# Attention of a three-layer kernel: chunks of 64 on quarter tiles, transposed output placed by copies, first loads by tensor

## The chip, the cores and the metric

One core of a Trainium2 chip runs the kernel. The time is the device time of one execution in microseconds (us). The engines are PE (TensorE, matrix products, with its weight loads shown apart as PEld), DVE (VectorE), ACT (ScalarE), POOL (GpSimd) and SP (SyncE, which issues all DMAs here).

## The reference

Three layers follow each other. The first is a gated linear attention with a state of 48 x 48 per head (4 batches, 8 heads, 768 steps); the other two are dense layers on its output, 3072 tokens of 384 values.

```
f = 1 / (1 + exp(-f_logit))
for t in range(768):
    state = f[:, :, t, :, None] * state + outer(k[:, :, t], v[:, :, t])
    y[:, :, t] = q[:, :, t] @ state
x = y, heads side by side                    # 3072 x 384
x = (h * tanh(softplus(h))) @ w_out          # h = x @ w_in, 384 -> 2048 -> 384
out = (sigmoid(x @ w_gate) * (x @ w_val)) @ w_out2   # 384 -> 1536 -> 384
```

The weights come as 64-bit floats and are turned into pairs of 32-bit parts on the chip; the inputs q, k, v, f as 32-bit.

## The kernel before, in words

**Attention.** A unit is four heads (two pairs, r = 0 and 1; in a pair one head lies on partitions 0 to 47, the other on 64 to 111) over half a sequence, 384 steps. There are 16 units; units 2j and 2j+1 make the x of block j, a block being 384 tokens. `unit(m)` (line 404) puts a unit's steps on a calendar of ticks: loads (`load_qkf`, `load_v`), the exponential of the forget logits and +1 (`s_exp`), the running product R of 1/f within a chunk of 128 steps by scans on VectorE (`s_scan`, six instructions), its logarithm and inverse on ScalarE (`s_lnexp`), the scaling of k and q by R and its inverse (`s_hat`), the scores of each chunk on PE (`p_scores`, per r) and their causal mask on VectorE (`s_mask`), the transposes of k (`p_kt`) and their copy out of PSUM (`s_kt`), the state that each chunk adds (`p_state`), the scan that carries it over chunks (`s_state`), the state's part of the output (`p_inter`), the chunk's own part (`p_intra`), and the copy of the output into `xtok`, tokens on partitions (`s_out`, lines 535 to 542).

**First dense layer.** `block1(j)` transposes `xtok` on PE (`p_xt`, nine 128 x 128 transposes a block), copies the result out of PSUM on ScalarE (`s_xt`), splits x into a high and a low part (`s_x`), and then does 16 hidden slices of 128: nine main products each into the hidden layer (`p_h`, tile h) and, 11 ticks later, nine out of it (`p_o`, tiles y0 to y2, from ghi and glo). Each main product is a 128 x 128 weight tile with 384 moving columns. One hidden slice is one tick; a block is 16 ticks. ScalarE evicts h and computes the activation in groups of four slices, VectorE helps.

**Weights.** `weights1` (line 643) loads and converts w_in in pairs of slices (buffers hs2, ghi1, glo1, z) and w_out in single slices (stg0, stg1, both): one or two ScalarE and four VectorE instructions each (`conversion`). `weights2` converts the second layer's weights between ticks 27 and 110 into DRAM (w2d) and loads them again when room is free. `block2` is the last layer.

**Order.** Every step has a tick and a priority (`at`). A planner (`_in_order`, with `_cost` for durations) fixes the order of all instructions from them: on each engine, the step that is ready and has the smallest (tick, priority) goes first. At run time each engine, and SP with all its DMAs, keeps that order. T0[m] is unit m's tick: -13, -9, 0, 4, then 8m - 23. All recorded instructions have line 926.

Of the kernel before, what the change touches and what calls it, by code (L numbers as in the profile page):

```python
# [20 lines left out]
C = 128  # L21
T = 384
# [70 lines left out]
def _cost(engine, method, args, kwargs):  # L93
# [215 lines left out]
def kernel(  # L309
# [53 lines left out]
    def flat(tag, n, dt=F32):  # L363

        return st(tag, [128, n if tag == "S" else 2 * T], dt)[:, 0:n]

# [8 lines left out]
    rb = st("rb", [128, 1])  # L375
# [3 lines left out]
    sc = st("sc", [128, 2, 2, D])  # L379
# [12 lines left out]
    def setup():  # L392
        nc.scalar.preload_act_table_set("natural_log_exp_and_others")
        nc.gpsimd.memset(rb.get(), RBIG)
# [3 lines left out]
        nc.gpsimd.affine_select(out=cm.get(), in_=cm.get(), pattern=[[1, C]], compare_op=ALU.is_ge, fill=0.0, base=0, channel_multiplier=-1)  # L398
        nc.vector.memset(fl.get(), 0.0)


    xtok = {}

    def unit(m):
# [8 lines left out]
        tR, tpf, *tA, tkt, tT = EARLY[m] if m < len(EARLY) else LATER  # L413
# [7 lines left out]
        def load_qkf():  # L421
            u["qkf"] = st(f"qkf{m % 2}", [128, 2, 3, T])
            sp.dma_start(out=u["qkf"], in_=qkf[n0 : n0 + 2].rearrange("r p i t -> p r i t"))
            u["q"], u["k"], u["f"] = (u["qkf"][:, :, i, :] for i in range(3))

        def load_v():
            u["vn"] = st("vn", [128, 2, T // 128, 2 * D])
            sp.dma_start(out=u["vn"], in_=vn[n0 : n0 + 2].rearrange("r p i d -> p r i d"))

        def s_exp():  # L430
            f = u["f"]
            act.activation(out=f, in_=f, func=AF.Exp, scale=-1.0)
            dve.tensor_scalar(out=f, in0=f, scalar1=1.0, scalar2=None, op0=ALU.add)
# [15 lines left out]
        def s_hat():  # L449
# [7 lines left out]
            pz = u["pz"] = flat("v6" if m == 1 else "S", 2 * D * NC).rearrange("p (r e c) -> p r e c", r=2, c=NC)  # L457
            pool.memset(pz[:, :, :, 0], 0.0)
            act.activation(out=pz[:, :, :, 1:NC], in_=pend[:, :, 0 : NC - 1].unsqueeze(2).to_broadcast([128, 2, D, NC - 1]), func=AF.Copy)

        def p_scores(r):
            ps = u["ps", r] = pst(pq, "s", [128, 2, 512])
            for i in range(NC):
                t = slice(i * C, (i + 1) * C)
                for hd, (_, rows_) in enumerate(heads):
                    pe.matmul(ps[:, hd, t], u["k"][rows_, r, t], u["q"][rows_, r, t], start=True, stop=True)

        def s_mask(r):
            A = u["A", r] = flat(tA[r], 2 * T).rearrange("p (h i t) -> p h i t", h=2, t=C)
            dve.tensor_tensor(  # L470
                out=A, in0=u["ps", r][:, :, 0:T].rearrange("p h (i t) -> p h i t", t=C),
                in1=cm.unsqueeze(1).unsqueeze(1).to_broadcast([128, 2, NC, C]), op=ALU.mult,
            )

        def p_kt(r):
            ps = u["pk", r] = pst(pa, "a", [128, T])
# [8 lines left out]
        def p_state():  # L485
            ps = u["pu"] = pst(pa, "a", [128, T])
            cols = ps[:, 0 : 2 * NC * D].rearrange("p (r e c) -> p r e c", r=2, c=NC)
            if half:
                for r in range(2):
                    pe.matmul(cols[:, r, :, 0], ident, sc[:, pp, r, :], start=r == 0, stop=False)  # L490
            for r in range(2):
                for i in range(NC):
                    for hd, (h, _) in enumerate(heads):
                        pe.matmul(
                            cols[h, r, :, i], u["kt"][:, r, C * i + 64 * hd : C * i + 64 * hd + 64], u["vn"][:, r, i, D * hd : D * hd + D],
                            start=not half and r == i == 0, stop=r == 1 and i == NC - 1,
                        )

        def s_state():
            n = 2 * NC * D  # L500
            t = u["t"] = flat(tT, n)
            dve.tensor_tensor_scan(
                out=t, data0=u["pz"].rearrange("p r e c -> p (r e c)"), data1=u["pu"][:, 0:n], initial=0.0, op0=ALU.mult, op1=ALU.add
            )
            t = u["t"] = t.rearrange("p (r e c) -> p r e c", r=2, c=NC)
            S = u["S"] = flat("S", 2 * (NC - 1) * D).rearrange("p (r c e) -> p r c e", r=2, e=D)
            dve.tensor_tensor(
                out=S, in0=t.rearrange("p r e c -> p r c e")[:, :, 0 : NC - 1, :],
# [3 lines left out]
        def s_carry():  # L512
            dve.tensor_tensor(
                out=sc[:, pp], in0=u["t"][:, :, :, NC - 1], in1=pend[:, :, NC - 1 : NC].to_broadcast([128, 2, D]), op=ALU.mult
            )

        todo = [(i, r) for r in range(2) for i in range(NC)]

        def p_inter():
            ps = u["py"] = pst(pq, "s", [128, 2, 512])  # L520
            inter = [x for x in todo if half or x[0]]
            for i, r in inter:
                for hd, (_, rows_) in enumerate(heads):
                    S = u["S"][rows_, r, i - 1, :] if i else sc[rows_, pp, r, :]
                    o = slice((2 * i + r) * D, (2 * i + r + 1) * D)
                    pe.matmul(ps[:, hd, o], u["q"][rows_, r, i * C : (i + 1) * C], S, start=(i, r) == inter[0], stop=False)

        def p_intra(r):
            ps = u["py"]
            for i in range(NC):  # L530
                for hd in range(2):
                    o = slice((2 * i + r) * D, (2 * i + r + 1) * D)
                    pe.matmul(ps[:, hd, o], u["A", r][:, hd, i, :], u["vn"][:, r, i, D * hd : D * hd + D], start=False, stop=(i, r) == todo[-1])

        def s_out():
            if pp == 0:
                xtok[j] = st("xtok", [128, T // 128, DM])
            to = xtok[j][:, :, 4 * D * pp : 4 * D * (pp + 1)].rearrange("p i (r h e) -> p i r h e", r=2, h=2)
            for hd in range(2):
                act.activation(  # L540
                    out=to[:, :, :, hd], in_=u["py"][:, hd, 0 : 2 * NC * D].rearrange("p (i r e) -> p i r e", r=2, e=D), func=AF.Copy, scale=-1.0,
                )

        o = OFFS[0 if m < 2 else 1 if m < 4 else 2]
        at(t0 - 4, 0, load_qkf)
        at(t0 + o[3], 0, load_v)
# [4 lines left out]
        at(t0 + o[4], 50, lambda: p_scores(0))  # L551
        at(t0 + o[4], 51, lambda: p_kt(0))
        at(t0 + o[4], 51.1, lambda: s_mask(0))
        at(t0 + o[4], 51.2, lambda: s_kt(0))
        at(t0 + o[5], 50, lambda: p_scores(1))
        at(t0 + o[5], 50, lambda: p_kt(1))
        at(t0 + o[5], 51.1, lambda: s_mask(1))
# [3 lines left out]
        late = 0 if m < 4 else 2  # L561
# [3 lines left out]
        at(t0 + o[8] + 0.5 * late, 52, lambda: p_intra(0))  # L565
        at(t0 + o[8] + late, 52, lambda: p_intra(1))
# [117 lines left out]
    xt, xf, xh, xl = {}, {}, {}, {}  # L684
# [6 lines left out]
    def block1(j):  # L691
        t0 = NF1 * j

        def p_xt(kc):
            ps = xt[j, kc] = pst(pa, "a", [128, T])
            for i in range(T // 128):
                t = slice(i * 128, (i + 1) * 128)
                pe.transpose(ps[:, t], xtok[j][:, i, kc * 128 : kc * 128 + 128], ident)

        def s_xt(kc):  # L700
            if kc == 0:
                xf[j] = st("y1s", [128, KC, T])
            act.activation(out=xf[j][:, kc, :], in_=xt[j, kc], func=AF.Copy)

# [7 lines left out]
        for kc in range(KC):  # L712
            at(t0 - 3 + kc, 54, lambda kc=kc: p_xt(kc))
            at(t0 - 2 + kc, 1, lambda kc=kc: s_xt(kc))
# [286 lines left out]
```

## Time and profile before

| | |
|---|---|
| median of 3 runs | 1049.8 us (1049.34 to 1050.55) |
| profiled execution | 1050.13 us, span 1048.4 us |
| PE busy in the span | 1006.4 us, 5922 matrix instructions |
| DVE, ACT busy | 519.2 and 541.3 us |
| DMA | 93.81 MB, 89 GB/s in the mean |

The profile is one execution. The span runs from its first to its last instruction, and the execution's own time is 1.7 us longer. Matrix products are pipelined and overlap; the time from one entry of the chain of waits to the next is what a step costs.

### The profile page before, as it was taken

To read this page: it belongs to the slowest core of one execution; us is meant where nothing else is said; L and a number is where in the kernel's file an instruction comes from. 1 tells how busy PE (TensorE), PEld (TensorE's weight loads), DVE (VectorE), ACT (ScalarE), POOL (GpSimd) and SP (SyncE) were. 2 spreads that over 40 slices of the span, in tenths; PEclk is the share of its full clock that TensorE was granted. 3 is DMA by queue.
4 is the path that set the end of the run, shared out by engine and by line. 5 is a ranking of instruction groups with operands and counts; after the bars stand their busy time and mean duration, and the time that the engine had idled before them with its cause. 6 is when DMAs were issued, how large, how long until landed. Compare 5 with 4: busy or idle time off the path is not lost.

```text
span 1048.4 us, 14376 instructions
## 1 busy us (share of the span) xinstructions
PE 1006.4 (96%) x5922; PEld 898.3 (86%) x5922; DVE 519.2 (50%) x806; ACT 541.3 (52%) x778; POOL 30.5 (3%) x44
## 2 busy tenths in 40 slices
PE   0799999999999999999999999999999999999996
PEld 0789999999999999999999888888888888888885
DVE  7789997786777878763333222222121121221221
ACT  5369888878787888766678312122122122211121
POOL 0000000000000000000011001001001001000000
PEclk9999999999999999999999999999999999999999
DMA  8225334544254444410247221001000000000001
GB/s 341 87 73 188 107 102 141 177 144 151 99 184 149 159 161 147 170 46 13 88 151 230 90 65 63 1 14 48 1 31 31 1 30 1 1 31 1 1 31 33
DMA packets 40041, 93.81 MB, mean 89 GB/s; under 512 B 3872, under 2 KB 15648, under 8 KB 39968
## 3 DMA queue, kind: packets, MB, share of 16 engines
q1 hardware_dynamic: 39968, 92.81, 26.1%
q8 instruction: 48, 0.79, 0.3%
q14 instruction: 25, 0.20, 0.1%
HBM read 69.21 MB, written 23.59 MB: 89 GB/s over the span
## 4 chain that ended last, share of the span: by engine, by line
PE 88%; DVE 5%; DMA 3%; ACT 2%; issue 1%; SPq 0%; DVEq 0%
PE y L926 31%; PE h L926 31%; PE s L926 18%; PE a L926 8%; DMA stg<-in_w_dram 2%; ACT z L926 1%; DMA w2d<-stg 1%; DVE w L926 1%; DVE v L926 1%; DVE hs L926 1%; DVE stg L926 0%; DVE qkf L926 0%; DMA hs<-in_w_dram 0%; DVE glo L926 0%; DVE R L926 0%
## 5 line engine op out<-in xcount | busy, mean ns | idle before, releaser
L926 PE MATMUL y<-ghi,v 128*128 128x384 f32 (+1 forms) x948 | 282.0, 352 | 0.0
L926 PE MATMUL h<-xs,w 128*128 128x384 f32 (+1 forms) x1260 | 255.3, 347 | 0.0
L926 ACT ACTIVATE hs<-h 128x384 f32<-128x384 f32 (+1 forms) x200 | 104.8, 524 | 288.1 <-PE h L926 287.3
L926 PEld LDWEIGHTS h<-xs,w 128*128 128x128 f32 x1260 | 220.1, 189 | 5.4
L926 PEld LDWEIGHTS y<-ghi,v 128*128 128x128 f32 x948 | 174.7, 188 | 11.0
L926 PE MATMUL y<-glo,v 128*128 128x384 f32 (+1 forms) x474 | 164.5, 347 | 0.0
L926 ACT ACTIVATE ghi<-hs 128x512 fp32r<-128x512 f32 (+1 forms) x104 | 87.9, 889 | 87.8 <-PE y L926 83.1
L926 DVE TENSOR_TENSOR glo<-hs,ghi 128x512 fp32r<-128x512 f32 (+1 forms) x104 | 101.7, 1015 | 60.9 <-ACT ghi L926 59.3
L926 DVE TENSOR_TENSOR hs<-hs,s 128x512 f32<-128x512 f32 x48 | 33.0, 687 | 168.4 <-PE s L926 151.6
L926 ACT ACTIVATE z<-z 128x1536 f32<-128x1536 f32 x64 | 94.9, 1482 | 14.0 <-DVE z L926 13.7
L926 PEld LDWEIGHTS y<-glo,v 128*128 128x128 f32 x474 | 89.1, 188 | 4.3
L926 DVE SCALAR_TENSOR_TENSOR hs<-z,hs 128x1536 f32<-128x1536 f32 x32 | 56.2, 1756 | 60.9 <-ACT z L926 60.9
L926 DVE TENSOR_TENSOR hs<-hs,a 128x512 f32<-128x512 f32 x24 | 16.5, 688 | 128.1 <-PE a L926 123.0
L926 PE MATMUL y<-ghi,w 128*128 128x512 f32 x180 | 60.5, 394 | 0.0
L926 PE MATMUL s<-qkf 48*128 48x128 f32 x384 | 33.6, 313 | 26.9 <-DVE qkf L926 25.8
L926 PEld LDWEIGHTS s<-qkf 48*128 48x128 f32 x384 | 27.0, 208 | 34.5 <-DVE qkf L926 25.8
L926 ACT ACTIVATE z<-z,fifth 128x1536 f32<-128x1536 f32 x32 | 50.3, 1571 | 0.2
L926 ACT ACTIVATE z<-hs 128x1536 f32<-128x1536 f32 x32 | 47.6, 1488 | 0.7
L926 PEld LDWEIGHTS s<-vn,A 128*128 128x128 f32 x360 | 46.4, 201 | 0.0
L926 DVE TENSOR_SCALAR z<-z 128x1536 f32<-128x1536 f32 x32 | 30.9, 965 | 29.8 <-ACT z L926 29.5
L926 PE MATMUL s<-vn,A 128*128 128x48 f32 x360 | 45.1, 279 | 0.0
L926 PEld LDWEIGHTS y<-ghi,w 128*128 128x128 f32 x180 | 33.8, 188 | 7.9
(244 smaller groups left out, 1404.5 us busy)
## 6 DMA issues: line engine op xcount, KB each, us to landing
qkf<-in_qkf_dram SPq DMA_DIRECT2D x16, 1152.0 KB, 5.3
stg<-in_w_dram SPq DMA_DIRECT2D x36, 384.0 KB, 3.2
w2d<-stg SPq DMA_DIRECT2D x36, 384.0 KB, 2.8
w<-w2d SPq DMA_DIRECT2D x16, 384.0 KB, 4.1
v<-w2d SPq DMA_DIRECT2D x14, 384.0 KB, 3.1
vn<-in_vn_dram SPq DMA_DIRECT2D x16, 288.0 KB, 3.2
y1d<-y1s SPq DMA_DIRECT2D x24, 192.0 KB, 2.7
stg<-in_w1o_dram SPq DMA_DIRECT2D x11, 384.0 KB, 3.8
```

Source lines behind the costliest of these rows:

```text
L926: issue(*map(_now, args), **{k: _now(x) for k, x in kwargs.items()})
```

## The change

Chunks are 64 steps rather than 128, so a unit has six per half sequence and row pair. Two neighbouring chunks (even and odd, `h`) lie in the two halves of the partitions. Every attention product works on 64 rows and 64 columns of the array, in an `order` in which successive products go to different quarters (inter: two of them in turn).

- `s_scan` is two scans instead of six; the restart at a chunk's first step comes from `m2`, into which ScalarE writes the first 1+exp(-f) of each chunk.
- Scores of both r share one PSUM tile, with one mask instruction.
- The state is copied out of PSUM by ScalarE, the carried state is added on VectorE rather than by identity products on PE, and the scan runs over 576 elements rather than 288.
- `p_inter` and `p_intra` give the output transposed (head dimension on partitions, steps along the row); weights of 64 columns reach 16 past a head's 48, for which zeros are kept (`s_pad`, one small identity product and a copy).
- `s_out` evicts the output transposed and puts each head's rows into `xf` by SP copies inside SBUF, five per unit, a head that crosses 128 rows in two. `p_xt` and `s_xt` go.
- q, k and f of a unit are three loads. For units 0 and 1 they are early: f0, k0, q0, f1, then the first weight pair, then k1, q1 and v; the other weight loads come after that. Unit 1 uses the PSUM tiles y0 to y2 and h, and +1 is on ScalarE for these two units.
- Later units start one tick later (8m - 22), and the wait between inter and intra is one tick rather than two.

```diff
-C = 128
+C = 64
...
-T0 = [-13, -9, 0, 4] + [8 * m - 23 for m in range(4, ND)]
-LATER = ("R", "pf", "A0", "A1", "pf", "R")
-EARLY = [("R", "pf", "A0", "A1", "v15", "v14"), ("v7", "v8", "v9", "v10", "v11", "v12"), LATER[:4] + ("v13", "v14"), LATER[:4] + ("v12", "v15")]
+T0 = [-13, -9, 0, 4] + [8 * m - 22 for m in range(4, ND)]
+LATER = ("R", "pf", "A0", "pf")
+EARLY = [LATER[:3] + ("v15",), ("v7", "v8", "v9", "v10"), LATER[:3] + ("v13",), LATER[:3] + ("v12",)]
...
-        rows_, cols = aps[1].shape
-        return 0.225 if rows_ == cols == 128 else 0.07 if rows_ == 128 else 0.145 if n == 128 else 0.125
+        return 0.035 if aps[1].shape[0] < 128 else 0.1
...
+        order = [(i, hd, h) for i in range(T // 128) for hd, h in ((0, 0), (1, 1), (0, 1), (1, 0))]
+        tR, tpf, tA, tkt = EARLY[m] if m < len(EARLY) else LATER
...
+        def load_qkf(part=None):
+            if part in (None, 2):
+                u["qkf"] = st(f"qkf{m % 2}", [128, 3, 2, T])
+                u["q"], u["k"], u["f"] = (u["qkf"][:, i] for i in range(3))
+            for i in (2, 1, 0) if part is None else (part,):
+                sp.dma_start(out=u["qkf"][:, i], in_=qkf[n0 : n0 + 2, :, i].rearrange("r p t -> p r t"))
...
+            act.activation(out=m2[:, :, :, 0], in_=chunks(f)[:, :, :, 0], func=AF.Identity, bias=1.0)
+            if m < 2:
+                act.activation(out=f, in_=f, func=AF.Identity, bias=1.0)
+            else:
+                dve.tensor_scalar(out=f, in0=f, scalar1=1.0, scalar2=None, op0=ALU.add)
...
+        def banks(kind):
+
+            if m == 1:
+                ps = [pst(py, f"y{i}", [128, T]) for i in range(2)] if kind != 1 else [pst(ph, "h", [128, T]) for i in range(2)]
+                return ps, None
+            ps = pst(pq, "s", [128, 2, 512])
+            return [ps[:, i, 0:T] for i in range(2)], ps[:, :, 0:T]
+
+        def both(ps, fn):
+
+            if ps[1] is not None:
+                fn(ps[1], slice(0, 2))
+            else:
+                for i in range(2):
+                    fn(ps[0][i].unsqueeze(1), slice(i, i + 1))
+
+        def bank():
+            return pst(py, "y2", [128, T]) if m == 1 else pst(pa, "a", [128, T])
...
-                for c in range(NC):
-                    t = slice(c * C, (c + 1) * C)
-                    dve.tensor_tensor_scan(
-                        out=u["R"][:, r, t], data0=u["f"][:, r, t], data1=rb.to_broadcast([128, C]), initial=1.0, op0=ALU.mult, op1=ALU.min
-                    )
+                dve.tensor_tensor_scan(
+                    out=u["R"][:, r], data0=u["f"][:, r], data1=m2[:, r].rearrange("p c t -> p (c t)"), initial=1.0, op0=ALU.mult, op1=ALU.min
+                )
...
+        def p_scores():
+            ps = u["ps"] = banks(0)
+            for r in range(2):
+                for i, hd, h in order:
+                    rows_ = heads[hd][1]
+                    t = slice((2 * i + h) * C, (2 * i + h + 1) * C)
+                    o = slice((3 * r + i) * C, (3 * r + i + 1) * C)
+                    pe.matmul(ps[0][hd][heads[h][0], o], u["k"][rows_, r, t], u["q"][rows_, r, t], start=True, stop=True)
+
+        def s_mask():
+            A = u["A"] = flat(tA, 2 * T).rearrange("p (h x t) -> p h x t", h=2, t=C)
+            both(u["ps"], lambda ps, hd: dve.tensor_tensor(
+                out=A[:, hd], in0=ps.rearrange("p h (x t) -> p h x t", t=C),
+                in1=cm.unsqueeze(1).unsqueeze(1).to_broadcast([128, hd.stop - hd.start, NC, C]), op=ALU.mult,
+            ))
...
+            ps = u["pu"] = banks(1)
+            for i, hd, h in order:
                 for r in range(2):
-                    pe.matmul(cols[:, r, :, 0], ident, sc[:, pp, r, :], start=r == 0, stop=False)
-            for r in range(2):
-                for i in range(NC):
-                    for hd, (h, _) in enumerate(heads):
-                        pe.matmul(
-                            cols[h, r, :, i], u["kt"][:, r, C * i + 64 * hd : C * i + 64 * hd + 64], u["vn"][:, r, i, D * hd : D * hd + D],
-                            start=not half and r == i == 0, stop=r == 1 and i == NC - 1,
-                        )
+                    o = slice((3 * r + i) * D, (3 * r + i + 1) * D)
+                    pe.matmul(
+                        ps[0][h][heads[hd][0], o], u["kt"][heads[h][0], r, 128 * i + 64 * hd : 128 * i + 64 * hd + 64],
+                        v_(h, r, i, hd)[:, 0:D], start=True, stop=True,
+                    )
+
+        def v_(h, r, i, hd):
+
+            a = (2 * (3 * r + i) + hd) * D
+            return u["vn"][heads[h][0], a : a + 64]
...
+            t = u["f"].rearrange("p r t -> p (r t)")[:, 0:n]
+            cols = t.rearrange("p (e x h) -> p h x e", h=2, x=NC)
+            both(u["pu"], lambda ps, h: act.activation(
+                out=cols[:, h], in_=ps[:, :, 0 : NC * D].rearrange("p h (x e) -> p h x e", e=D), func=AF.Copy
+            ))
+            T_ = u["t"] = t.rearrange("p (e r c) -> p e r c", r=2, c=NC)
+            was = sc[:, 0 : 4 * D].rearrange("p (a r e) -> p a e r", a=2, r=2)[:, pp]
+            if half:
+                dve.tensor_tensor(out=T_[:, :, :, 0], in0=T_[:, :, :, 0], in1=was, op=ALU.add)
+            dve.tensor_tensor_scan(out=t, data0=u["pz"].rearrange("p e r c -> p (e r c)"), data1=t, initial=0.0, op0=ALU.mult, op1=ALU.add)
...
+            ps = u["py"] = banks(2)
+            begun = set()
+            for r in range(2):
+                for i, hd, h in order:
+                    c = 2 * i + h
+                    if c or half:
+                        o = slice((3 * r + i) * C, (3 * r + i + 1) * C)
+                        t = slice(c * C, (c + 1) * C)
+                        pe.matmul(ps[0][h][heads[hd][0], o], S_(hd, r, c), u["q"][heads[hd][1], r, t], start=(h, hd) not in begun, stop=False)
+                        begun.add((h, hd))
+            u["0"] = bank()[:, 0 : 64 - D]
+            pe.matmul(u["0"], ident, sc[:, 4 * D :], start=True, stop=True)
+
+        def s_pad():
+            dve.tensor_copy(out=u["vn"][:, 4 * T // 128 * D :], in_=u["0"])
...
+            for r in (1, 0):
+                for i, hd, h in order[::-1]:
+                    o = slice((3 * r + i) * C, (3 * r + i + 1) * C)
+                    pe.matmul(
+                        ps[0][h][heads[hd][0], o], v_(h, r, i, hd), u["A"][heads[h][0], hd, 3 * r + i, :],
+                        start=False, stop=r == i == 0,
+                    )
...
-                xtok[j] = st("xtok", [128, T // 128, DM])
-            to = xtok[j][:, :, 4 * D * pp : 4 * D * (pp + 1)].rearrange("p i (r h e) -> p i r h e", r=2, h=2)
-            for hd in range(2):
-                act.activation(
-                    out=to[:, :, :, hd], in_=u["py"][:, hd, 0 : 2 * NC * D].rearrange("p (i r e) -> p i r e", r=2, e=D), func=AF.Copy, scale=-1.0,
-                )
+                xf[j] = st("xf", [128, KC, T])
+            xT = rows(flat(tA, 2 * T))
+            cols = xT.rearrange("p r (i h t) -> p h (r i) t", h=2, t=C)
+            both(u["py"], lambda ps, h: act.activation(
+                out=cols[:, h], in_=ps.rearrange("p h (x t) -> p h x t", t=C), func=AF.Copy, scale=-1.0
+            ))
+            for r in range(2):
+                for hd in range(2):
+                    a = (4 * pp + 2 * r + hd) * D
+                    e = 0
+                    while e < D:
+                        kc, row = divmod(a + e, 128)
+                        n = min(D - e, 128 - row)
+                        sp.dma_start(out=xf[j][row : row + n, kc, :], in_=xT[64 * hd + e : 64 * hd + e + n, r, :])
+                        e += n
...
+        if m < 2:
+            for i, tick in ((2, -21 + m / 10), (1, -20.99 + 0.94 * m), (0, -20.98 + 0.94 * m)):
+                at(tick, 0, lambda i=i: load_qkf(i))
+            at(-20.04 + m / 100, 0, load_v)
+        else:
+            at(t0 - 4, 0, load_qkf)
+            at(t0 + o[3], 0, load_v)
...
+        at(t0 + o[8], 54, s_pad)
+        at(t0 + o[8] + late, 55 if m < 4 else 52, p_intra)
...
-        pairs = {t: (-20 + i / 10, e) for i, (t, e) in enumerate((("hs2", 15), ("ghi1", 9), ("glo1", 11), ("z", 2.5)))}
-        singles = {t: (-19 + i / 10, 99) for i, t in enumerate(("stg0", "stg1", "both"))}
+        pairs = {t: (-20.5 + i, e) for i, (t, e) in enumerate((("hs2", 15), ("ghi1", 9), ("glo1", 11), ("z", 2.5)))}
+        singles = {t: (-18 + i / 10, 99) for i, t in enumerate(("stg0", "stg1", "both"))}
...
-        def p_xt(kc):
-            ps = xt[j, kc] = pst(pa, "a", [128, T])
-            for i in range(T // 128):
-                t = slice(i * 128, (i + 1) * 128)
-                pe.transpose(ps[:, t], xtok[j][:, i, kc * 128 : kc * 128 + 128], ident)
-
-        def s_xt(kc):
-            if kc == 0:
-                xf[j] = st("y1s", [128, KC, T])
-            act.activation(out=xf[j][:, kc, :], in_=xt[j, kc], func=AF.Copy)
```

## Rows read from the trace of the kernel before

**Rows 1.** The page: busy time of each engine, then tenths in 40 slices.

```profile
PE 1006.4 (96%) x5922; PEld 898.3 (86%) x5922; DVE 519.2 (50%) x806; ACT 541.3 (52%) x778; POOL 30.5 (3%) x44
...
PE   0799999999999999999999999999999999999996
...
DVE  7789997786777878763333222222121121221221
...
GB/s 341 87 73 188 107 102 141 177 144 151 99 184 149 159 161 147 170 46 13 88 151 230 90 65 63 1 14 48 1 31 31 1 30 1 1 31 1 1 31 33
```

**Rows 2.** Stage busy us: PE, PEld, DVE, ACT, POOL; clock, DMA share, GB/s.

```profile
0.00:64.00 64.00, 31.58 (x213) 27.66 (x214) 50.08 (x89) 29.89 (x47) 1.73 (x13) 1.00 0.54 199
64.00:124.90 60.90, 60.90 (x495) 57.47 (x495) 55.64 (x94) 50.19 (x75) 0.70 (x3) 1.00 0.33 109
124.90:171.00 46.10, 46.10 (x324) 44.72 (x323) 41.42 (x70) 40.59 (x58) 0.23 (x1) 1.00 0.44 152
100.00:300.00 200.00, 200.00 (x1466) 191.84 (x1466) 165.48 (x271) 166.72 (x239) 1.57 (x6) 1.00 0.42 142
```

**Rows 3.** The chain of waits at the start: start us, us, what.

```profile
25.75 1.68 PE s L926 x12
...
64.13 6.15 PE h L926 x27
```

**Rows 4.** The start in order of time: start us, us, engine, line, operation.

```profile
4.28 1.03 SPq L926 DMA_DIRECT2D qkf<-in_qkf_dram  x2
...
16.20 0.83 ACT L926 ACTIVATE qkf<-qkf 128x768 f32<-128x768 f32 x1
...
18.34 1.99 DVE L926 TENSOR_TENSOR_SCAN R<-qkf,rb 128x128 f32<-128x128 f32 x6
```

**Rows 5.** PE in order of time, 50 to 70 us.

```profile
52.55 5.35 PE L926 MATMUL s<-vn,v 128*128 128x48 f32 x24
```

**Rows 6.** The chain of waits between 205 and 300 us.

```profile
206.12 0.87 PE s L926 x12
206.98 1.79 PE y L926 x9
208.77 0.33 PE a L926 x3
...
215.17 1.21 PE a L926 x28
...
221.28 1.57 PE h L926 x9
...
224.43 1.47 PE s L926 x24
...
229.24 1.27 PE s L926 x12
...
252.67 0.84 PE a L926 x24
...
257.18 1.02 PE s L926 x16
```

**Rows 7.** VectorE and ScalarE by shape: busy us, mean ns of one.

```profile
L926 DVE TENSOR_TENSOR_SCAN R<-qkf,rb 128x128 f32<-128x128 f32 x90 | 30.4, 403 | 0.0
L926 DVE TENSOR_TENSOR A<-s,cm 128x768 f32<-128x768 f32 x30 | 28.6, 952 | 5.5 <-PE s L926 5.4
...
L926 DVE TENSOR_TENSOR_SCAN R<-S,a 128x288 f32<-128x288 f32 x12 | 9.0, 747 | 3.6 <-PE a L926 3.6
...
L926 ACT ACTIVATE hs<-h 128x384 f32<-128x384 f32 x128 | 61.7, 482 | 34.2 <-PE h L926 33.4
```

**Rows 8.** DMA issues: KB each, median us from issue to landing.

```profile
y1d<-y1s SPq DMA_DIRECT2D x24, 192.0 KB, 2.7
...
hs<-in_w_dram SPq DMA_DIRECT2D x4, 768.0 KB, 4.5
...
out_dram<-z SPq DMA_DIRECT2D x12, 64.0 KB, 1.7
```

More of the change, by code (lines that the diff above doesn't have):

```diff
@@ L374 @@
     cm = st("cm", [128, C])
-    rb = st("rb", [128, 1])
+    m2 = st("m2", [128, 2, NC, C])
     fifth = st("fifth", [128, 1])
@@ L393, in setup @@
         nc.scalar.preload_act_table_set("natural_log_exp_and_others")
-        nc.gpsimd.memset(rb.get(), RBIG)
+        nc.gpsimd.memset(m2.get(), RBIG)
+        nc.gpsimd.memset(sc.get(), 0.0)
         nc.gpsimd.memset(fifth.get(), 0.2)
@@ L419, in rows @@
             return ap.rearrange("p (r t) -> p r t", r=2)
[L421 to L424, printed above, removed]
+        def load_qkf(part=None):
[4 more added lines that the diff above has]
+                sp.dma_start(out=u["qkf"][:, i], in_=qkf[n0 : n0 + 2, :, i].rearrange("r p t -> p r t"))
         def load_v():
-            u["vn"] = st("vn", [128, 2, T // 128, 2 * D])
-            sp.dma_start(out=u["vn"], in_=vn[n0 : n0 + 2].rearrange("r p i d -> p r i d"))
+            n = 4 * T // 128 * D
+            u["vn"] = flat("v5" if m == 1 else "vn", n + 64 - D)
+            sp.dma_start(out=u["vn"][:, 0:n].rearrange("p (r i d) -> p r i d", r=2, d=2 * D), in_=vn[n0 : n0 + 2].rearrange("r p i d -> p r i d"))
         def s_exp():
@@ L456, in s_hat @@
             dve.tensor_scalar(out=pend, in0=chunks(pf)[:, :, :, C - 1], scalar1=-1.0, scalar2=None, op0=ALU.mult)
-            pz = u["pz"] = flat("v6" if m == 1 else "S", 2 * D * NC).rearrange("p (r e c) -> p r e c", r=2, c=NC)
+            pz = u["pz"] = flat("v6" if m == 1 else "S", 2 * D * NC).rearrange("p (e r c) -> p e r c", r=2, c=NC)
             pool.memset(pz[:, :, :, 0], 0.0)
-            act.activation(out=pz[:, :, :, 1:NC], in_=pend[:, :, 0 : NC - 1].unsqueeze(2).to_broadcast([128, 2, D, NC - 1]), func=AF.Copy)
-        def p_scores(r):
-            ps = u["ps", r] = pst(pq, "s", [128, 2, 512])
-            for i in range(NC):
[L464 to L472, printed above, removed]
-            )
+            act.activation(out=pz[:, :, :, 1:NC], in_=pend[:, :, 0 : NC - 1].unsqueeze(1).to_broadcast([128, D, 2, NC - 1]), func=AF.Copy)
+        def p_scores():
[12 more added lines that the diff above has]
+            ))
         def p_kt(r):
-            ps = u["pk", r] = pst(pa, "a", [128, T])
+            ps = u["pk", r] = bank()
             for i in range(T // 128):
@@ L499, in s_state, with S_ @@
+        def v_(h, r, i, hd):
+            a = (2 * (3 * r + i) + hd) * D
+            return u["vn"][heads[h][0], a : a + 64]
+        def S_(hd, r, c):
+            a = (5 * r + c - 1) * D if c else (2 * pp + r) * D
+            return (u["S"] if c else sc)[heads[hd][1], a : a + 64]
         def s_state():
             n = 2 * NC * D
[L501 to L504, printed above, removed]
@@ L513, in s_carry @@
             dve.tensor_tensor(
-                out=sc[:, pp], in0=u["t"][:, :, :, NC - 1], in1=pend[:, :, NC - 1 : NC].to_broadcast([128, 2, D]), op=ALU.mult
+                out=sc[:, 0 : 4 * D].rearrange("p (a r e) -> p a e r", a=2, r=2)[:, pp], in0=u["t"][:, :, :, NC - 1],
+                in1=pend[:, :, NC - 1].unsqueeze(1).to_broadcast([128, D, 2]), op=ALU.mult,
             )
-        todo = [(i, r) for r in range(2) for i in range(NC)]
         def p_inter():
[L520 to L526, printed above, removed]
@@ L560, in unit @@
         at(t0 + o[7], 2, s_state)
-        late = 0 if m < 4 else 2
+        late = 0 if m < 4 else 1
         at(t0 + o[8], 52, p_inter)
@@ L798, in load_y @@
         def load_y():
-            two = st("xtok", [128, 2, T2])
+            two = st("xf", [128, 2, T2])
             yf[j] = [two[:, 0], two[:, 1], st("y1s", [128, T2])]
@@ L809, in s_ysplit @@
                 else:
-                    parts[j] = [st(tag, [128, T2], F32R) for tag in ("R", "pf", "A0", "A1", "stg0", "stg1")]
+                    parts[j] = [st(tag, [128, T2], F32R) for tag in ("R", "pf", "A0", "m2", "stg0", "stg1")]
             yh[j, kc], yl[j, kc] = parts[j][2 * kc : 2 * kc + 2]
```

44 lines of the change are left out of this document (13 added, 31 removed).

## The prediction

> **What bounds the kernel now.** I read the page first. PE is busy for 96% of the span, with slices of 0 and 7 tenths at the start and 9 from then on; VectorE stands at 7 to 9 tenths through most of the first half and then falls to 3 and less [rows 1]. So there is a start without main products, a long stretch bound by PE with little to spare beside it, and a second half with PE alone. The stage table prices this: VectorE works 50.1 of the first 64 us while PE has 31.6, and from 64 us on PE is busy for all of each stretch [rows 2]. The chain of waits gives the border: the first product of the first hidden layer (PE h) begins at 64.1 us, and PE's first work of all, scores, only at 25.75 [rows 3].
>
> Why so late? In order of time the two qkf loads are issued at 4.28, behind six weight loads. Unit 0's exponential comes at 16.20, its running product (R) at 18.34 [rows 4]. The page's first slice moves 341 GB/s [rows 1]; the six weight loads (3 x 768 and 3 x 384 KB, 3.5 MB) and one qkf load (1.2 MB) need 13.8 us at that, so 16.2 is about when q, k and f of unit 0 can be in.
>
> All of this start runs with PE at the lower of its two levels, 1.2 GHz. The granted-clock column says 1.00 even there [rows 2], but the durations don't: 24 intra-chunk instructions take 5.35 us at 52.55, twelve take 1.27 later, 223 against 106 ns each [rows 5, 6].
>
> **PE, per unit (16 units of four heads).** One fp32 call is two MATMUL instructions in the trace: six calls show as x12. Steady prices [rows 6]: scores 2 x 0.87; k transposes 2 x 0.33; state 0.84 without and 1.21 with the carried state, mean 1.03; products of the state into the output (inter) 1.02 and 1.47, mean 1.25; intra 2 x 1.27. The nine transposes of x in a block are 3 x 0.33, so 0.5 per unit. The group of nine main products behind small tiles takes 1.79 in place of 1.57: 0.2 each after scores (twice), state and inter. Sum 8.5 us. A block has 32 groups of nine, 50.2 us at 1.57, and two units: 67.2 us.
>
> Afterwards scores, state and intra are 24 calls each, 48 instructions on 64 rows and 64 columns, and four quarters of the array take turns. No row shows a quarter. The nearest is state, 128 rows by 64 columns on two halves: 24 in 0.84, 35 ns each, so a half comes round every 70 ns. If a quarter comes round in the same 70, four give 17.5 ns: 0.84 per step. The upper end is the row itself, 35: 1.68. I take 17.5, because the moving width grows only from 48 to 64 while the number of tiles doubles. Inter uses two quarters only, since a head's rows of S and of its output lie on the same partitions: 44 instructions in the mean at 35 ns, 1.54; ends 17.5 (0.77) and 61 ns (1.47/24, two row groups with 128 columns: 2.7). The pad product is one more call, priced as one of the two that make 1.21 of 0.84: 0.19. k transposes stay, 0.66; four switches of 0.2, 0.8; the transposes of x go. Sum 3 x 0.84 + 1.54 + 0.19 + 0.66 + 0.8 = 5.7, so 2.8 us less per unit; with both ends, from 3.6 less to 0.9 more.
>
> The Trainium skill speaks against this halving: "TensorE: Matmul & The Clock Gate", section "Wait — 56ns, not 53.3ns?", says that start to start never drops below about 25 ns however small N is. No row here goes below 35, so none contradicts it. By that figure three steps would be an estimated 48 x 0.025 = 1.2 each, and a unit would lose 1.7 rather than 2.8.
>
> **VectorE and ScalarE, per unit** [rows 7]. VectorE: the mask is one instruction of 0.95 rather than two, -0.95; R two scans for six over the same elements, 2 x (403 + 256 x 2.15 = 953 ns) for 1.99 [rows 4], -0.1; the state scan has 576 for 288 elements at (747-403)/160 = 2.15 ns, +0.62; S 288 elements more at the mask's 1.24 ns, +0.36; adding the carried state (every other unit) and the pad copy, two small ones, +0.3. Net +0.2. ScalarE, at 482/384 = 1.26 ns an element: the state out of PSUM, 576 elements, +0.72; the pz broadcast, 288 more, +0.36; the first column of each chunk and 192 output elements more, +0.4; evictions of x, 1.5 x 0.48 less. Net +0.7 at most. Between 100 and 300 us ScalarE has 166.7 of 200, VectorE 165.5 [rows 2]: 28.0 of 33.6 per unit for ScalarE, then 28.7 of 30.8. Hidden, but tight; I charge 3 us in total for lost cover, between 0 and half of the steady gain.
>
> **Moved loads and copies.** Each unit's output is placed by five SBUF-to-SBUF copies, and qkf comes in three loads for one: seven more issues on SP, 0.5 us each (two in 1.03 [rows 4]), 3.5 us per 30 of a queue that holds w2 loads and stores behind them. Each copy waits there for ScalarE's eviction, and a late w2 load would show as VectorE waiting for stg. No row has such a copy; 1.7 us (64 KB to DRAM) and 4.5 (768 KB in) bound it, and the 192 KB store's 2.7 is nearest in kind [rows 8]. A unit's output comes at tick 8m-12, the split that reads it at tick 16j, so the later unit has four ticks, at 3.8 us each, for 3 us of copies: covered. At the start alone, for unit 1, it is on the path, in place of three rounds of transpose and eviction ahead of the h products at 64.13 [rows 3]; I count it even.
>
> **The start.** f of unit 0 goes first: 384 KB is 1.15 us at 341 GB/s, on top of the 2.2 that a 768 KB load of 4.5 has besides its transfer [rows 8], so it lands at about 4.2. Then the exponential and +1 on ScalarE (0.83 each [rows 4]) to 6; two scans to 7.9; the products with R (0.95 each, as the mask), with unit 1's scans among them: scores at about 13.5 rather than 25.75. From there four PE steps per unit at half speed (1.7 us each), 3 us of VectorE per unit and ScalarE's copies, with PSUM banks of its own for unit 1, which no longer waits for unit 0's output: unit 1's output near 33, copies 3, split, first PE h near 40. That is 24 us earlier. If the chain keeps its length of 47.9 (16.20 to 64.13), it is 12 earlier.
>
> But work put off comes back. By 171 us VectorE has 147 us of durations at 253 instructions [rows 2], and neighbours overlap: by about 0.08 us each, I estimate, which leaves 127. With 6 us empty at the start it can't be there before 133. PE: 40, plus the 107 it spends from 64 to 171, less 4.5 units x 2.8 = 134. Two engines with nothing spare don't mesh; I take 8 us of waits: 142, 29 earlier (12 if only the shift stays, 38 without waits).
>
> **Sum**, against the profiled execution's 1050.1 (span 1048.4; the median of the runs is 1049.8, so 0.3 lower): start to 171 us -29; ten later units x 2.8, -28; lost cover +3; the second half and the tail, without attention, 0. Result 996.
>
> **Rivals.**
> (a) Quarters don't double the rate: scores, state and intra at 35 ns each. For: it is the only row with 64-column tiles. Against: that row had two tiles, not four. A unit takes 3 x 1.68 + 1.54 + 1.65 = 8.2, 0.3 less than now: steady -3, start -27, 1020. By the floor that the Trainium skill states (the clock gate page, the section named above) the estimate lies between the two, at about 1007.
> (b) Debt at the start: PE begins early and then waits for weights, so that 12 remain. For: VectorE's 133 equals PE's 134. Against: so far the same work fits with time to spare. 1050 - 12 - 28 + 2 = 1012.
> (c) ScalarE becomes the bound until 500 us: its 28.7 of 30.8 with waits holds a unit's half block at 32.2. Half of the steady gain, 1050 - 27 - 14 = 1009.
> (d) Slower: column groups don't overlap and a quarter costs the inter row's 61 ns. 188 x 0.061 + 1.65 = 13.1 per unit, 4.6 more than now, x 14 units = +64, with 12 won at the start: about 1102. With 20 won at the start it decides from (8.5 + 2.0 - 1.65)/188 = 47 ns per instruction on. Against: state's 35 ns on column halves.
> (e) It does not do what it says: f is issued first but ScalarE's order still has weights ahead, and PE is no quicker: 1050.
>
> **Chances.** Forecast 0.45, (a) 0.23, (b) 0.13, (c) 0.11, (d) 0.06, (e) 0.02. The forecast's own range is 976 (start 38, 3.6 per unit) to 1006. With (a) to (c) the range is 970 to 1028. Less than 0.2% (2 us) can't be told from no change here; faster 0.92, same 0.02, slower 0.06.
>
> **What would show it.** PE h begins near 40 us, unit 0's exponential near 4.2. The small-tile steps show x48 in 0.84 us (right) or 1.7 (a) in the chain; a block of two units takes 61.6 us rather than 67.2; PE's waits between 40 and 140 us sum to some 8 us. Wrong if PE waits more than 10 us between 171 and 560, or if copies into xf appear as what the split or a mask waits for.

## The result, and the profile after

The changed kernel takes 1016.33 us (median of 4, 1015.38 to 1017.17) against 1049.85: ratio 0.968, interval 0.9663 to 0.9697. Faster, as forecast, by 33.5 us rather than 54. The profiled execution took 1017.17 with a span of 1015.5, 33.0 less than the one before. All times below are of that execution where a profile or a trace is read, else medians.

The page of the changed kernel, busy times and slices of 25.4 us:

```profile
PE 963.6 (95%) x7386; PEld 852.3 (84%) x7386; DVE 522.8 (51%) x749; ACT 553.4 (54%) x774; POOL 38.3 (4%) x62
...
PE   3687899999999999999999999999999999999996
...
DVE  6888997989788878874433221221221222122121
...
PEclk9598999999999999999999999999999999999998
...
GB/s 256 192 134 148 79 164 156 148 145 139 180 172 180 167 148 147 162 175 108 100 195 170 67 65 32 1 32 32 1 32 31 1 32 1 1 32 1 0 32 35
```

PE works earlier, 3 and 6 tenths in the first two slices for 0 and 7 [rows 1], but it is full only from the sixth slice on, where before it was from the third, and its clock row dips to 5 tenths in the second. The stage table has stretch, its us, then busy us of PE, PEld, DVE, ACT and POOL, clock, DMA share, GB/s. 42.3 is the first product of the first hidden layer (PE h), 116.0 and 184.3 the beginnings of the second and third block, 246.8 to 308.8 a whole later block:

```profile
26.00:42.40 16.40, 10.01 (x187) 8.81 (x182) 13.29 (x22) 8.99 (x14) 0.38 (x2) 0.51 0.75 244
...
42.30:116.00 73.70, 60.07 (x705) 53.51 (x704) 65.66 (x99) 56.04 (x80) 0.78 (x4) 0.88 0.41 126
116.00:184.30 68.30, 65.13 (x684) 62.00 (x682) 60.16 (x94) 59.22 (x85) 1.15 (x4) 0.98 0.45 143
246.80:308.80 62.00, 61.69 (x674) 58.75 (x673) 52.27 (x77) 55.31 (x75) 1.66 (x4) 1.00 0.49 159
```

Before, the first block went from 64.1 to 124.9, 60.9 us with PE never idle [rows 2]; the third block began at 190.7, and the next ones took 67.5 to 68.8 us each. So the lead is 21.8 us at PE h, 8.9 at the second block, 6.4 at the third, and from there it grows by 5 to 6 us a block to 33.

The start of the changed kernel in order of time (start us, us, engine, line, operation, in brackets idle time and who ended it):

```profile
0.81 1.98 SPq L975 DMA_DIRECT2D qkf<-in_qkf_dram  x4
...
4.14 0.84 ACT L975 ACTIVATE qkf<-qkf 128x768 f32<-128x768 f32 x1 [2.05 <-DMA qkf<-in_qkf_dram]
...
6.28 1.81 DVE L975 TENSOR_TENSOR_SCAN R<-qkf,m 128x384 f32<-128x384 f32 x2 [5.34 <-ACT qkf L975]
...
16.18 1.56 PE L975 MATMUL s<-qkf 48*64 48x64 f32 x48 [3.39 <-DVE qkf L975]
...
36.59 0.87 ACT L975 ACTIVATE v<-y 128x384 f32<-128x384 f32 x2 [4.11 <-PE y L975]
...
37.49 3.51 SPq L975 DMA_DIRECT2D xf<-v  x5
...
44.72 1.12 ACT L975 ACTIVATE xs<-xf 128x384 fp32r<-128x384 f32 x2 [1.44 <-DMA xf<-v]
```

Exponential and scan stand where the working put them, 4.2 and 6 [rows 4 has 16.20 and 18.34]. Scores come at 16.18, not 13.5, and unit 1's output at 36.6, not 33. Its five copies are issued over 3.5 us, and the split of x on ScalarE waits for them until 44.72.

PE from 42 to 70 us and in a later unit:

```profile
42.29 1.31 PE L975 MATMUL h<-xs,w 128*128 128x384 f32 x3
45.30 6.78 PE L975 MATMUL h<-xs,w 128*128 128x384 f32 x24 [1.69 <-ACT xs L975]
52.00 0.93 PE L975 MATMUL s<-qkf 48*64 48x64 f32 x48
52.86 3.40 PE L975 MATMUL h<-xs,w 128*128 128x384 f32 x18
56.19 0.99 PE L975 MATMUL s<-vn,v 64*64 64x48 f32 x48
57.11 5.14 PE L975 MATMUL h<-xs,w 128*128 128x384 f32 x27
...
251.45 1.38 PE L975 MATMUL s<-qkf,S 48*64 48x64 f32 x40
252.76 0.40 PE L975 MATMUL a<-sc,ident 128*128 128x16 f32 x2
...
318.59 0.93 PE L975 MATMUL s<-A,vn 64*64 64x64 f32 x48
319.45 1.83 PE L975 MATMUL h<-xs,w 128*128 128x384 f32 x9
```

From one start to the next: scores 0.86 us (52.00 to 52.86) and intra 0.86 (318.59 to 319.45) for 48 instructions, 18 ns each; state 0.92 for 48 (56.19 to 57.11), 19 ns; inter 1.31 for 40, 33 ns; the pad product 0.25 (from 252.76 to the next product, at 253.01). [Rows 6] had 2 x 0.87 and 2 x 1.27 for scores and intra. After 45.30 the first 24 products need 6.7 us, 279 ns each; 18 of the same take 3.33 at 52.86, 185 each. PE's granted clock had fallen to 1.2 GHz at 26.2 us (0.51 in the stage row up to 42.4), after a wait from 23.6 to 25.8, and rose again at 50.1, with PE at work since 45.3. The 9 of the clock row in the first slice is not what PE ran at: 48 scores last 1.56 us at 16.18 and 0.93 at 52.00.

### The profile page after: what moved, and what is told of

Its sections match the earlier page's. It is cut to its first block, busy times and chain, and to the rows that moved or that the text cites. A ratio compares the mean times of both kernels' runs of the same rounds, so it can differ in the third digit from the quotient of the medians.

```text
span 1015.5 us, 17476 instructions
## 1 busy us (share of the span) xinstructions
PE 963.6 (95%) x7386; PEld 852.3 (84%) x7386; DVE 522.8 (51%) x749; ACT 553.4 (54%) x774; POOL 38.3 (4%) x62
## 4 chain that ended last, share of the span: by engine, by line
PE 57%; DVE 0%; ACT 0%; issue 0%
PE y L975 21%; PE h L975 20%; PE s L975 11%; PE a L975 5%; DVE hs L975 0%; ACT z L975 0%; ACT hs L975 0%; ACT pf L975 0%; ACT ghi L975 0%
## 5 line engine op out<-in xcount | busy, mean ns | idle before, releaser
L975 PEld LDWEIGHTS h<-xs,w 128*128 128x128 f32 x1260 | 224.7, 192 | 13.8 <-ACT hs L975 3.6
L975 ACT ACTIVATE ghi<-hs 128x512 fp32r<-128x512 f32 (+1 forms) x104 | 88.0, 890 | 87.1 <-PE y L975 73.7
L975 PE MATMUL y<-glo,w 128*128 128x512 f32 x90 | 35.4, 393 | 0.0
L975 PE MATMUL a<-ident,qkf 128*128 128x128 f32 x90 | 16.6, 298 | 17.1 <-DVE fl L975 9.2
L975 DVE TENSOR_TENSOR_SCAN R<-qkf,m 128x384 f32<-128x384 f32 x30 | 28.2, 950 | 5.5 <-ACT qkf L975 5.3
L975 PEld LDWEIGHTS a<-ident,qkf 128*128 128x128 f32 x90 | 11.7, 150 | 19.8 <-issue 9.2
```

The source lines that it names most:

```text
L975: issue(*map(_now, args), **{k: _now(x) for k, x in kwargs.items()})
```

## Experiments

Four theories, numbered 1 to 4 in what was expected. Debt (1): VectorE's conversions of the first layer's weights and the waits around them set the first 180 us, whatever the start. Carried (2): the early start reaches the end and something else is lost. Copies (3): the SBUF copies on SP's queue and their latency hold the start. Clock (4): the stretches at 1.2 GHz cost the time.

**Loads put back.**

```
-        if m < 2: ...            # f, k, q of units 0 and 1 at ticks -21 to -20, v at -20
+        at(t0 - 4, 0, load_qkf)  # as for all units; the weight loads at -20 and -19
+        at(t0 + o[3], 0, load_v)
```

> The changed kernel with the loads of the first two units and of the first weights put back to their places of before. Theory 1 (debt: VectorE's weight conversions and the waits around them set the first 180 us, whatever the start): the early loads are worth little by then, 1018 to 1022 us. Theory 2 (the early start is carried to the end): 12 us or more are lost, 1028 or above.

1022.38, ratio 0.9744 (0.9725 to 0.9763), so the early loads are worth 6 to 7 us of the medians. Its PE, in order of time:

```profile
57.66 1.65 PE L970 MATMUL h<-xs,w 128*128 128x384 f32 x4
...
116.69 1.55 PE L970 MATMUL h<-xs,w 128*128 128x384 f32 x8
```

PE h begins 15.4 us later than in the changed kernel, the second block 0.7 us later. The lead is gone within one block: debt. The profiled execution, 1017.96, is the fastest of its four (the others 1022.3 to 1024.7), so where the others lose 4 to 6 us more is not shown.

**Only the loads moved**, in the kernel before.

```
...
-        at(t0 - 4, 0, load_qkf)
-        at(t0 + o[3], 0, load_v)
+        if m < 2:
+            for i, tick in ((2, -21 + m / 10), (1, -20.99 + 0.94 * m), (0, -20.98 + 0.94 * m)):
+                at(tick, 0, lambda i=i: load_qkf(i))
+            at(-20.04 + m / 100, 0, load_v)
...
+        pairs = {t: (-20.5 + i, e) for i, (t, e) in enumerate(...)}
```

> The kernel before with only the loads moved (f, k, q apart and early, first weights behind them, unit 1's v in its own tile). Theory 1 (debt): PE h begins some 10 us earlier but the total falls by 2 to 6 us, 1044 to 1048. Theory 2 (carried): 1038 or below.

1043.93, ratio 0.9947 (0.9929 to 0.9965): 5.6 us. Debt again, inside its range. From both sides the early loads bring 5 to 7 us.

**Less VectorE work.** Two of the four VectorE instructions of each first-layer conversion are left out.

```
             act.activation(out=m.bitcast(F32), in_=w[:, :, :, 1].bitcast(F32), func=AF.Abs, ...)
+            if spill is None: return
             dve.tensor_scalar(out=k, ...)
             dve.scalar_tensor_tensor(out=k, ...)
...
```

> The changed kernel without two of the four VectorE instructions of each first-layer weight conversion, some 22 us of VectorE in all (the converted weights are then not the reference's). Theory 1 (debt): PE's waits between 42 and 184 us, 16.8 us, and the stretches at 1.2 GHz in it shrink by more than half; 1000 to 1006. Theory 3 (SP's copies and their latency hold the start): 1013 to 1016.

1002.63, ratio 0.9546 (0.9529 to 0.9563), 14 us below the changed kernel for 22 us of VectorE work. The stage table of its own first two blocks:

```profile
43.40:107.00 63.60, 57.30 (x705) 52.12 (x704) 52.15 (x72) 54.45 (x78) 0.78 (x4) 0.95 0.41 134
107.00:170.80 63.80, 63.22 (x682) 60.32 (x682) 52.40 (x75) 58.84 (x84) 0.80 (x4) 1.00 0.48 153
```

The two blocks take 63.6 and 63.8 us rather than 73.7 and 68.3, which is the whole gain. PE's idle time in them falls from 13.6 + 3.2 to 6.3 + 0.6 us and the clock rises from 0.88 to 0.95 and from 0.98 to 1.00, with nothing done for the clock. Debt is confirmed as the larger part, and the lower clock is mostly its consequence.

**One copy per unit in place of five.**

```
-            for r in range(2): ...   # five copies
+            sp.dma_start(out=xf[j][:, pp : pp + 2, :], in_=xT)
```

> The changed kernel with one SBUF copy of 128 rows per unit in place of five (the rows then don't lie where the reference has them). Theory 3 (copies): unit 1's output reaches the split 4 us earlier and masks no longer wait for the buffer, 1008 to 1011. Theory 1 (debt): 1014 to 1016.

1011.26, ratio 0.9625 (0.9602 to 0.9649): 5.1 us, so the copies theory holds for a part. The copies of the changed kernel, KB each and median us from issue to landing (xf<-v is unit 1):

```profile
xf<-A SPq DMA_DIRECT2D x45, 72.0 KB, 3.0
...
xf<-A SPq DMA_DIRECT2D x15, 48.0 KB, 2.6
...
xf<-v SPq DMA_DIRECT2D x3, 72.0 KB, 5.3
xf<-v SPq DMA_DIRECT2D x1, 48.0 KB, 6.2
xf<-v SPq DMA_DIRECT2D x1, 24.0 KB, 6.6
```

In the median the other copies take the 3 us that was taken; those of unit 1 take 4.8 to 7.0, above the bound of 4.5 [rows 8], and those of unit 2, at 67.8, 4.4 to 6.3. Both go out 2.5 us after three qkf loads (35.0 and 65.3). These loads were not taken away, so why the copies are slower is not shown.

The gain is not won ahead of the first block. With one copy, unit 1's output has landed at 41.6 rather than 45.2 us, but PE does scores first and runs h from 45.1, where the changed kernel runs it without a break from 45.3. The second, third and fourth blocks begin 2.2, 4.0 and 6.0 us earlier. What the copies hold there is VectorE: the tile A, from which a unit's output is copied, is the one that the next mask writes. The masks of the changed kernel that wait for copies, in order of time:

```profile
74.92 0.96 DVE L975 TENSOR_TENSOR A<-s,cm 128x768 f32<-128x768 f32 x1 [1.62 <-DMA xf<-A]
...
173.05 0.96 DVE L975 TENSOR_TENSOR A<-s,cm 128x768 f32<-128x768 f32 x1 [2.26 <-DMA xf<-A]
```

These are 3.9 us in two waits; with one copy per unit a single one of 1.7 is left. The kernel before has no such wait: its output went from PSUM into `xtok`. Whether these waits account for all of the 5 us is not shown.

**Both.**

> The changed kernel without two of four VectorE conversion instructions of the first-layer weights and with one copy per unit in place of five (neither the converted weights nor the rows of x are the reference's). If VectorE's conversions (14 us) and the copies (5 us) are two separate parts of what the forecast missed, they add: 996 to 999 us. If both only make room for the same wait, 1001 to 1003.

996.48, ratio 0.9496 (0.9459 to 0.9534): the two add, 19.9 us. PE h begins later than in the changed kernel, at 48.5, and the second block still at 101.4: the first block takes 52.9 rather than 73.7 us. An early first product alone says little.

**The subtraction of the low weight parts on GpSimd**, 24 instructions.

```
-                dve.tensor_tensor(out=lo, in0=pair(x), in1=hi.bitcast(F32), op=ALU.subtract)
+                pool.tensor_tensor(out=lo, in0=pair(x), in1=hi.bitcast(F32), op=ALU.subtract)
```

> The changed kernel with the subtraction that makes the low part of each first-layer weight on GpSimd in place of VectorE (24 instructions, some 14 us of VectorE by its durations). Theory 1 (debt on VectorE): the ratio of the run without two conversion steps, 14 us won for 22 taken off, gives 9 us: 1005 to 1010. Rival (the low parts only come later from the slower engine, or the two engines slow each other): 1014 or above.

1017.1, ratio 0.9685 (0.9669 to 0.9701): nothing. The rival was right. VectorE between 42 and 116 us, first the kernel with GpSimd at work, then the changed kernel (busy us, mean ns of one):

```profile
L975 DVE SCALAR_TENSOR_TENSOR hs<-z,hs 128x1536 f32<-128x1536 f32 x3 | 6.8, 2266 | 0.0
...
L975 DVE SCALAR_TENSOR_TENSOR stg<-v 128x384 int32<-128x384 int32 x5 | 6.0, 1202 | 0.0
```

```profile
L975 DVE SCALAR_TENSOR_TENSOR hs<-z,hs 128x1536 f32<-128x1536 f32 x3 | 5.3, 1755 | 0.1
...
L975 DVE SCALAR_TENSOR_TENSOR stg<-v 128x384 int32<-128x384 int32 x6 | 3.3, 548 | 0.0
```

The same instructions are longer on VectorE, 1202 for 548 ns, and its busy time in that stretch rises from 65.7 us in 99 instructions to 72.8 in 87. The mean hides two kinds: the one at 71.23, beside a GpSimd subtraction from 71.07 to 72.99, takes 2.17 us, the one at 74.26, with GpSimd idle, 0.55. PE h begins 6.3 us later than in the changed kernel, and the first two blocks are 7.0 us shorter. Work was moved, load was not.

**PE kept busy ahead of the first block.**

```
+            def p_fill():                       # unit 1, behind p_intra
+                ps = pst(pa, "a", [128, T])
+                for _ in range(5):
+                    pe.matmul(ps, ident, u["vn"][:, 208:592], start=True, stop=True)
```

> The changed kernel with five products of 384 columns that nobody reads, behind unit 1's last product, so that PE is at work between 36 and 43 us while it would wait for the copies of unit 1's output. Theory 4 (the lower clock costs the time): the first products of the hidden layer run at 2.4 GHz and 3 to 4 us stay won, 1012 to 1013. Theory 1 (debt): they run at 2.4 GHz and the total stays within 2 us of the changed kernel.

1014.38, ratio 0.9662 (0.9646 to 0.9678), and the same ratio when it was run again (1014.31):

> The changed kernel with the five unread products again, beside the one with unit 4 later, for a comparison on one chip: 1013 to 1016.

It is 1.9 us below the changed kernel, and the intervals overlap. The stretch at 1.2 GHz ends at 39.7 rather than 50.1, another comes from 46.4 to 49.8, and the second block begins at 114.1. The mean clock of the first block's stretch (42.3 to 116) rises from 0.88 to 0.93, some 3.7 us of full clock, for those 1.9. At most a small part is clock in its own right.

**Both, GpSimd and the filling products.**

> Both edits, subtraction on GpSimd and the five products. Theory 1 (debt): with VectorE relieved an earlier clock is of some use: 1003 to 1009, at most 3 us below the run with GpSimd alone. Theory 4 (clock): the two gains add, 1002 or below.

1017.11, ratio 0.9689 (0.9665 to 0.9713). Both theories missed: nothing is left of either.

**The five products, and unit 4 two ticks later.**

```
-T0 = [-13, -9, 0, 4] + [8 * m - 22 for m in range(4, ND)]
+T0 = [-13, -9, 0, 4, 12] + [8 * m - 22 for m in range(5, ND)]
```

> The changed kernel with the five unread products of the run before and unit 4 two ticks later (12 in place of 10), which takes its VectorE work (some 8 us) out of the first block and puts it where VectorE is busy for 88% rather than 90. If VectorE's load in the first block is what holds it, 3 us are won on the run with the five products alone: 1010 to 1012. If the order of the work there doesn't matter as long as the sum is the same, 1014 to 1015.

1016.01, ratio 0.9682 (0.9669 to 0.9695), 1.7 us above the five products alone. Missed, and the premise was not met: VectorE is busy for 65.1 us in the first block where the run with the five products alone has 65.6, so other work came in for what was taken out. The second block begins 1.1 us earlier and the third at 182.6 against 182.7. So this run does not say what less VectorE work in the first block alone would give.

**Products sorted by quarter.**

```
-        order = [(i, hd, h) for i in range(T // 128) for hd, h in ((0, 0), (1, 1), (0, 1), (1, 0))]
+        order = [(i, hd, h) for hd, h in ((0, 0), (1, 1), (0, 1), (1, 0)) for i in range(T // 128)]
```

> The changed kernel with each attention step's products sorted by quarter of the array, so that successive ones go to the same quarter. If a quarter comes round in 70 ns (the working of the prediction), a step of 48 takes 3.4 us rather than 0.86 and inter 3.1 rather than 1.54: 9 us more per unit, some 1150 us. If only the issue sets the pace, nothing changes, 1016.

1058.02 (two executions), ratio 1.0073 (1.0049 to 1.0097), slower than the kernel before by 8 us but far from 1150. PE there:

```profile
272.60 1.43 PE L975 MATMUL s<-qkf,S 48*64 48x64 f32 x40
273.96 0.40 PE L975 MATMUL a<-sc,ident 128*128 128x16 f32 x2
...
277.54 1.75 PE L975 MATMUL s<-A,vn 64*64 64x64 f32 x48
279.23 0.97 PE L975 MATMUL h<-xs,w 128*128 128x384 f32 x4
...
287.25 1.75 PE L975 MATMUL s<-qkf 48*64 48x64 f32 x48
288.93 0.44 PE L975 MATMUL y<-ghi,v 128*128 128x384 f32 x1
...
296.08 2.42 PE L975 MATMUL s<-vn,pf 64*64 64x48 f32 x48
298.43 0.45 PE L975 MATMUL y<-ghi,v 128*128 128x384 f32 x1
```

In scores and intra one quarter alone takes an instruction every 35 ns (1.69/48), four in turn every 18. State takes 49 ns (2.35/48) rather than 19; why it is slower than the other two is not shown. Inter hardly changes, 34 ns (1.36/40) for 33. Neither reading held: a quarter's turn is not 70 ns, and where four quarters take turns the order does matter, by a factor of two and more.

**Inter in another order**, so that the two row halves don't write the same PSUM bank one after the other.

```
+            banked = [(i, hd, h) for two in (((0, 0), (1, 1)), ((0, 1), (1, 0))) for i in range(T // 128) for hd, h in two]
...
-                for i, hd, h in order:
+                for i, hd, h in banked:
```

> The changed kernel with the products of the state into the output (inter) in another order: first those that write bank 0 from the lower rows and bank 1 from the upper, then the others, so that a product of one row half does not directly follow one of the other half into the same bank. If two quarters can't run faster than one (32 ns per instruction in either order), nothing changes: 1014 to 1018. If it was the shared bank that kept them apart, the step falls from 1.54 to about 0.9 us per unit, 10 units: 1008 to 1011.

1016.01, ratio 0.9669 (0.9639 to 0.9698), and the step is the same:

```profile
249.66 1.38 PE L976 MATMUL s<-qkf,S 48*64 48x64 f32 x40
250.97 0.39 PE L976 MATMUL a<-sc,ident 128*128 128x16 f32 x2
```

1.31 us for 40 in both kernels. It is not the bank. Two quarters in turn, at 33 ns, do hardly better than one alone at 34 to 35; what holds them is open.

## Why the prediction was right or wrong

**PE per unit: right in size, by a wrong mechanism.** Forecast for scores and intra 0.84, measured 0.86; state 0.84, measured 0.92; inter 1.54 at 35 ns, measured 33 ns; pad 0.19, measured 0.25; a block 61.6 us, measured 62.0 (246.8 to 308.8) against 67.5 before. From the third block on, the lead grows from 6.4 to 33.0, 26.6 us for the ten units, where the sum had -28 and +3 for cover. Rival (a), 35 ns, is refuted by the rows. So is the floor of about 25 ns that the Trainium skill states in "TensorE: Matmul & The Clock Gate", section "Wait — 56ns, not 53.3ns?": 18 ns between instructions on four quarters; with one quarter, at 35, nothing here contradicts it. But that the halving of state's row by "a half comes round every 70 ns" came out was luck: sorted by quarter, one quarter alone takes 35 ns in scores and intra and 49 in state, and two in turn take 33. Why four in turn take 18 is not shown. Rival (a)'s own sum was too low: its start of -27 keeps about 2.5 us for each of 4.5 units that (a) denies them; without these it is some 1030 rather than 1020.

**The start: the step that failed.** "8 us of waits: 142, 29 earlier" is the term. The lead at the third block is 6.4 us, 22.6 less. PE h itself began at 42.3 for 40, with 1.7 us more of waiting at 45.3. Then PE idled 16.8 us up to 184.3, twice the 8, and ran at a mean clock of 0.88 over 73.7 us and 0.98 over 68.3, which is 8.8 + 1.4 = 10.2 us of full clock that the sum didn't have at all. 2.3 + 8.8 + 10.2 is 21.3 of the 22.6. That is an account of PE's time and not of causes: a wait that ends when VectorE is done gets longer when PE runs faster.

What stands behind both is VectorE, and the step that had it wrong is its floor of 133. "147 us of durations" less an overlap of "about 0.08 us each" takes the overlap off twice. The 50.1, 55.6 and 41.4 of the stage table [rows 2] are busy time, in which overlapping neighbours count once; the durations of these instructions sum to 164. In the kernel before, in order of time and then as a stage row:

```profile
102.14 0.95 DVE L926 TENSOR_TENSOR qkf<-pf,qkf 128x768 f32<-128x768 f32 x1
103.01 0.16 DVE L926 TENSOR_SCALAR pend<-pf 128x6 f32<-128x6 f32 x1
103.08 0.55 DVE L926 SCALAR_TENSOR_TENSOR both<-v 128x384 int32<-128x384 int32 x1
```

```profile
102.14:103.55 1.41, 1.41 (x10) 1.41 (x9) 1.41 (x4) 1.41 (x2) 0.00 (x0) 1.00 1.01 380
```

The three durations sum to 1.66 us, the stage row has 1.41 for VectorE (its fourth instruction begins at 103.55). So the floor by the same working is 147 + 6 = 153 rather than 133, and VectorE was the later of the two engines by 19 us, not PE's equal. What came can be read where the same main products are through PE (some 260 into the hidden layer and 160 out of it). The rows are of the kernel before, the changed kernel, the one with less VectorE work and the one with GpSimd:

```profile
0.00:171.10 171.10, 138.68 (x1029) 129.95 (x1029) 147.25 (x251) 120.67 (x179) 2.67 (x17) 1.00 0.44 154
0.00:167.10 167.10, 126.82 (x1593) 114.98 (x1594) 143.06 (x218) 125.08 (x179) 4.99 (x25) 0.89 0.51 165
0.00:152.80 152.80, 123.12 (x1590) 112.89 (x1591) 121.56 (x170) 124.88 (x182) 4.62 (x25) 0.98 0.54 179
0.00:167.40 167.40, 127.77 (x1590) 115.76 (x1591) 151.39 (x194) 124.77 (x181) 50.44 (x49) 0.87 0.51 165
```

The forecast had this point at 142, that is 127 us of VectorE's work and 15 without. It came at 167.1, with 143.1 of work and 24.0 without: 16 of the 25 us missed here are work (the 20 of overlap, less 4 that the change takes off VectorE) and 9 are idle time. VectorE is busy for 29.6 of the 42.3 us before PE h, so it is idle for 12.7 there rather than 6, and for 8.0 in the first block, in part for copies (below). Without 22 us of conversions the point comes 14.3 us earlier, and most of the clock comes back. With GpSimd at work VectorE is busy for 151.4 us on the way to it, though 24 instructions are no longer its own. Rival (b) named this, "PE begins early and then waits for weights", and gave it 0.13 and 12 us; the early loads were worth 5 to 7. Its 1012 was still too low, because the chain's shift of 12 was held to be safe.

**Copies: "covered", and at the start "I count it even".** Five copies rather than one cost 5.1 us. The sum had them at nothing: it priced the way to the split, in ticks, and a mask that must wait for the copies out of its tile was not in it. The prediction's own sign of being wrong, "if copies into xf appear as what the split or a mask waits for", did appear: 1.4 us ahead of a split and 3.9 ahead of masks. Unit 1's copies also took 4.8 to 7.0 us, outside the bounds, but the run with one copy shows no gain ahead of the first block.

**Cover (c).** (c) did not come: ScalarE at 55.3 of 62.0 leaves PE 0.3 us idle in a later block, and PE's waits between 171 and 560 sum to 2.3 us, where 3 were charged and more than 10 would have spoken against the forecast. Between 40 and 140, where some 8 us of waits were expected, PE is idle for 15.9.

**The whole.** The profiled execution is 21 us above the forecast, outside the forecast's own range of 976 to 1006 and inside the one of 970 to 1028 that takes in the rivals. The steady part was forecast right and the start was not. That the kernel without 22 us of conversions and with one copy lands on 996 is no proof that 996 was to be had: it leaves work out.

The kernel with five unread products, 1014.3 twice, is the fastest that computes the whole; against the changed kernel its gain of 2 us is not beyond the intervals.

## What to carry to other kernels

When a start is made earlier, price the stretch behind it by every engine's work up to the point where the lead is counted, not by the chain that was shortened: 15 us of lead were gone one block later. Find out first whether a table's busy time already leaves overlap out: taking it off twice made VectorE look 20 us shorter here. When a tile gets a second reader, ask who writes it next: the copies out of A held up masks. PE's waits of 16.8 us came with 10 us of lower clock, but winning back some of the clock alone gave 2 us at most, so look for the cause of the waits. And an engine that is idle is no relief if its work makes the loaded one slower: measure both.

## What the runs showed of the hardware

- Products on 64 x 64 quarters follow each other every 18 ns when four quarters take turns (state, with 48 columns, 19), 33 ns with two on the diagonal, and 35 ns on one alone in scores and intra, 49 in state.
- With GpSimd subtracting beside it, a VectorE instruction of 548 ns took 1202 in the mean of five, and 2.17 us where one lay beside a subtraction; one of 1755 took 2266. Scans kept their duration in that stretch (951 and 940 ns), but one at 38.32 us, beside a subtraction, took 2.49.
- SBUF-to-SBUF copies of 24 to 72 KB took 2.5 to 3.0 us to land in the median, 4.8 to 7.0 for unit 1 and 4.4 to 6.3 for unit 2; an issue held SP for 0.59 us in the median (0.51 to 1.54), against 0.37 for a load of weights.
